# Another order list for an attention and two feed-forward blocks, and the first pair loaded in two parts

## The chip, the cores and the metric

The kernel runs on one core of a Trainium2 chip. The core has TensorE (matrix products and transposes, results in PSUM), VectorE, ScalarE and GpSimd, and SyncE, which here only issues transfers between HBM and the on-chip memory. Each engine takes its instructions from its own queue in order and waits on semaphores for the others. The metric is the device time of the launch in microseconds. The kernel before takes 390.04 us in the median of three runs (389.51 to 390.77).

## The reference

There are 2 sequences of 448 tokens and 12 heads of width 64, all in float32; the weights come as float64.

```
scores = q @ k.T / 8, causal mask, softmax          # per batch and head
x   = (softmax @ v), heads side by side             # 2 x 448 x 768
xp  = x shifted by one token
xk  = mu_k*x + (1-mu_k)*xp ;  xr = mu_r*x + (1-mu_r)*xp
k   = relu(xk @ w_k) ;  v = k*k @ w_v               # 768 -> 1024 -> 768
r   = sigmoid(xr @ w_r) ;  x2 = r*v                 # 768 -> 768
h   = relu(x2 @ w_in)                               # 768 -> 1024
y   = (h * sigmoid(conv3(h, conv_w))) @ w_out       # 1024 -> 768
```

## The kernel before, in words

The attention works on 12 pairs of heads, six per batch. For pair i the steps are: `Lk` and `Lv` (loads of q and k, and of v), `kqT` (14 transposes on TensorE, 7 chunks of 64 tokens of q and of k), `kC` (the two copies out of PSUM), `sc.c` (scores of the query block c, for both heads), `red.c.j` (mask, minimum and scaling on VectorE, head j), `exp` (ScalarE), `rec` (reciprocals of the sums, VectorE), `norm` (scaling by them), `T.a` and `T.b` (transposes of the probabilities), `C.xx` (their copies out of PSUM), `V.kc` (products with v) and `out` (the copy of the result into `xT`).

The linear layers multiply float32 numbers as three products of a high and a low part (`mm3`, L64 to L67). So each activation and each weight slice is split: `mP` and `mD` mix a pair's output with its shifted copy, `mH` and `mL` make its high and low part (`xr`); `kx:P D H L` are the same steps for `xk`. A weight slice of 128 columns comes as float64 and is made float32 by five steps: `wE:L` is its load, `a` runs on ScalarE, `b` to `e` on VectorE (`b` on GpSimd where marked), then `h` and `l` give the two parts. `w0` to `w5` are the slices of w_r, `w6` to `w8` the first three of w_k, named wk0 to wk2 in the profile. There are two raw buffers for such loads; one is free again after step `e`. `pr e.b.c` is one product of slice e with chunk c of batch b, `sr` copies a finished pr result out of PSUM. `E0` and `E1` are the products of the first w_k slice for the two batches, `E2` and `E3` of the second.

All of this up to E3 stands in one list of tokens, `ORDER`, written out by hand or by a search outside the kernel. The loop over it issues each token's instructions in turn, and each engine but SyncE keeps that order exactly; the transfers that SyncE issues keep it among themselves. So a token is held up by whatever stands before it on its own engine. A suffix `/p`, `/a` or `/v` says GpSimd, ScalarE or VectorE. `W0` and `W*n` are matmuls of an identity with itself whose result is never read.

q and k of two pairs fit on chip (`qks` has two buffers): the load of pair i+2 waits for `kqT` of pair i. v has four buffers.

After E3 the other w_k slices, then w_v, w_in and w_out follow in loops (`token_mm`), where the order on each engine is left to the framework's scheduler. `take()` (called once for each slice) issues the conversion of coming slices and returns the next that is ready.

Of the kernel before, what the change touches and what calls it, by code (L numbers as in the profile page):

```python
# [19 lines left out]
def kernel(  # L20
# [233 lines left out]
    class Job:  # L254
        def __init__(self, i):
            self.i, self.b, self.hp = i, i // NPAIR, i % NPAIR
            self.T, self.p, self.s = {}, {}, {}
            self.scored = 0
# [6 lines left out]

        def Lk(self):
            t = self.raw = qks.get(self.i, self.name("rqk"))
            for src, dst, e in ((q, t[:LO], nc.sync), (k, t[LO:], nc.sync if self.i else nc.scalar)):
                for j in range(2):
                    in_order(e.dma_start(  # L270
                        out=dst[:, :, j], in_=src[self.b, 2 * self.hp + j].rearrange("(c p) d -> p c d", p=LO)
                    ))

        def Lv(self):
            t = self.v = vs.get(self.i, self.name("rv"))
            for j in range(2):
                x = v[self.b, 2 * self.hp + j]
                in_order(nc.sync.dma_start(out=t[:, :NB, j], in_=x[:MAIN].rearrange("(c p) d -> p c d", p=P)))
                in_order(nc.sync.dma_start(out=t[LO:, NB, j], in_=x[MAIN:]))

        def kqT(self, _):
            t = self.raw
            pt = {n: bank(self.name(n), 1) for n in "qk"}
            for c in range(S // LO):
                for n, r in (("q", slice(0, LO)), ("k", slice(LO, P))):
                    nc.tensor.transpose(
                        pt[n][:, c * LO:(c + 1) * LO], t[r, c].rearrange("p h d -> p (h d)"), ident[r, r]
                    )
            qks.put(self.i)

        def kC(self, eng, n):
            self.T[n] = t = Ts[n].get(self.i, self.name(f"{n}T"))
            copy(eng, t, used(self.name(n))[:, :S])
# [171 lines left out]
    class Slice:  # L465
# [325 lines left out]
```

## Time and profile before

| | |
|---|---|
| median of three runs | 390.04 us |
| the profiled execution's own time | 390.61 us |
| its span, first to last instruction | 388.7 us |
| TensorE busy, mean granted clock | 366.4 us, 0.987 of 2.4 GHz |
| VectorE, ScalarE, GpSimd busy | 300.5, 228.3, 128.8 us |

All durations below are from this one execution. Matmuls overlap in their pipeline, so a row's duration of one matmul is longer than the distance to the next; a busy TensorE is one that has no gap.

### The profile page before, as it was taken

Reading aid. Unit: us, or ns where it says so; the run is one execution under the profiler, and the core shown is the slowest. Engines: PE = TensorE matmul, PEld = TensorE weight load, DVE = VectorE, ACT = ScalarE, POOL = GpSimd, SP = SyncE. Lnnn points to the kernel's source line nnn. Section 1 sums busy time; section 2 is a strip of 40 time slices with the busy share of each in tenths; the row PEclk is TensorE's granted clock in tenths of the full one; section 3 lists DMA queues with packets and bytes.
Section 4 is the critical chain, followed back from the end, with each engine's and each line's share of the span. In section 5 each row is a group of like instructions: output and inputs, shape, how many; then the busy total and the mean of one; then the engine's idle time right before and its main releaser. Section 6 shows DMA issues by size and latency. Waiting matters only on the chain.

```text
span 388.7 us, 6581 instructions
## 1 busy us (share of the span) xinstructions
PE 366.4 (94%) x2374; PEld 315.5 (81%) x2374; DVE 300.5 (77%) x576; ACT 228.3 (59%) x488; POOL 128.8 (33%) x172
## 2 busy tenths in 40 slices
PE   7886999899896998999999899999999999999996
PEld 6445665576665897999999699999999999999996
DVE  2884999999898899888899799999999999500000
ACT  3984999779724425776778745553777667403111
POOL 2361799786986854100000000000134344300000
PEclk9996999999999999999999899999999999999999
DMA  5548755252213032445535443445521300004111
GB/s 118 126 98 206 193 118 124 80 128 83 83 51 110 3 97 70 160 162 164 193 133 189 142 155 109 146 154 163 162 83 44 118 2 1 2 0 143 41 61 42
DMA packets 60541, 41.36 MB, mean 106 GB/s; under 512 B 34616, under 2 KB 59484, under 8 KB 60508
## 3 DMA queue, kind: packets, MB, share of 16 engines
q1 hardware_dynamic: 59580, 40.71, 35.6%
q8 instruction: 19, 0.31, 0.3%
q10 hardware_dynamic: 928, 0.23, 0.3%
q14 instruction: 14, 0.11, 0.1%
HBM read 38.17 MB, written 2.75 MB: 105 GB/s over the span
## 4 chain that ended last, share of the span: by engine, by line
PE 54%; DVE 19%; DMA 10%; POOL 6%; ACT 6%; issue 3%; SPq 2%; POOLq 0%; ACTq 0%; DVEq 0%
PE pout L66 5%; PE ph L67 5%; PE ph L65 5%; PE ph L66 5%; PE pout L67 5%; PE pout L65 5%; PE pv L66 4%; PE pv L67 4%; PE pv L65 4%; PE s L303 4%; DVE m L415 3%; PE po L383 3%; DMA rqk<-in_k_dram 2%; DVE e L315 2%; POOL m L71 2%
## 5 line engine op out<-in xcount | busy, mean ns | idle before, releaser
L727 POOL TENSOR_TENSOR cv<-cv,hT 128x448 f32<-128x448 f32 x16 | 21.7, 1359 | 156.8 <-ACT cv L726 156.8
L71 POOL TENSOR_SCALAR p<-p,st 128x128 f32<-128x128 f32 (+3 forms) x69 | 40.4, 600 | 32.6 <-DVE st L333 18.9
L324 ACT ACTIVATE p<-e,st 128x384 f32<-128x384 f32 (+3 forms) x84 | 44.0, 527 | 4.4 <-DVE st L315 3.2
L315 DVE CUSTOM_DVE_ANT_0 e<-s,mask 128x256 f32<-128x256 f32 (+3 forms) x84 | 34.6, 444 | 3.9 <-PE s L303 3.3
L303 PE MATMUL s<-kT,qT 64*128 64x128 f32 (+3 forms) x192 | 35.8, 460 | 0.4 <-DVE pt L78 0.4
L756 ACT ACTIVATE osb<-pout 128x384 f32<-128x384 f32 x14 | 6.8, 491 | 40.0 <-PE pout L67 38.8
L415 DVE SCALAR_TENSOR_TENSOR m<-xT,mu,m 128x448 f32<-128x448 f32 x24 | 24.5, 1030 | 4.8 <-POOL m L71 3.5
L383 PE MATMUL po<-pt,rv 128*64 128x448 f32 (+3 forms) x192 | 26.4, 389 | 0.8 <-issue 0.8
L303 PEld LDWEIGHTS s<-kT,qT 64*128 64x128 f32 (+1 forms) x192 | 15.7, 179 | 10.6 <-DVE st L315 3.6
L383 PEld LDWEIGHTS po<-pt,rv 128*64 128x64 f32 (+1 forms) x192 | 12.9, 135 | 13.4 <-issue 8.3
L66 PE MATMUL pout<-wo_t,g 128*128 128x384 f32 x49 | 16.4, 335 | 0.0
L67 PE MATMUL pout<-wo_t,g 128*128 128x384 f32 x49 | 16.4, 335 | 0.0
L65 PE MATMUL pout<-wo_t,g 128*128 128x384 f32 x49 | 16.4, 334 | 0.0
L324 ACT ACTIVATION_READ_ACCUMULATOR p<-e,st 128x1 f32 x84 | 16.1, 191 | 0.0
L90 DVE TENSOR_TENSOR g<-cv,g 128x448 fp32r<-128x448 f32 x16 | 11.6, 725 | 3.7 <-ACT g L86 3.7
L71 POOL TENSOR_SCALAR m<-xT,mu 128x448 f32<-128x448 f32 x16 | 14.0, 879 | 1.1 <-DVE xr L90 0.7
L66 PE MATMUL pout<-wo_u,g 128*128 128x384 f32 x42 | 14.1, 336 | 0.0
L65 PE MATMUL pout<-wo_u,g 128*128 128x384 f32 x42 | 14.1, 335 | 0.0
L67 PE MATMUL pout<-wo_u,g 128*128 128x384 f32 x42 | 14.0, 334 | 0.0
L723 DVE SCALAR_TENSOR_TENSOR cv<-hT,cw,cv 128x448 f32<-128x448 f32 x16 | 13.6, 850 | 0.1
L90 POOL TENSOR_TENSOR xr<-m,xr 128x448 fp32r<-128x448 f32 x10 | 13.0, 1301 | 1.5 <-ACT xr L86 1.2
L722 DVE SCALAR_TENSOR_TENSOR cv<-hT,cw,cv 128x448 f32<-128x448 f32 x16 | 13.0, 812 | 0.4 <-ACT cv L721 0.3
(523 smaller groups left out, 1267.3 us busy)
## 6 DMA issues: line engine op xcount, KB each, us to landing
rqk<-in_q_dram SPq DMA_DIRECT2D x24, 112.0 KB, 3.0
out_dram<-osb SPq DMA_DIRECT2D x14, 192.0 KB, 1.9
rqk<-in_k_dram SPq DMA_DIRECT2D x22, 112.0 KB, 3.0
rv<-in_v_dram SPq DMA_DIRECT2D x24, 96.0 KB, 2.8
wv0raw<-in_moe_w_v_dram SPq DMA_DIRECT2D x1, 1024.0 KB, 5.0
wv1raw<-in_moe_w_v_dram SPq DMA_DIRECT2D x1, 1024.0 KB
wv2raw<-in_moe_w_v_dram SPq DMA_DIRECT2D x1, 1024.0 KB
wv3raw<-in_moe_w_v_dram SPq DMA_DIRECT2D x1, 1024.0 KB
```

Of the source, the lines that this page charges most:

```text
L65: nc.tensor.matmul(ps_out, lh, rh, start=first, stop=False)
L66: nc.tensor.matmul(ps_out, lh, rl, start=False, stop=False)
L67: nc.tensor.matmul(ps_out, ll, rh, start=False, stop=last)
L71: nc.gpsimd.tensor_scalar(out_, in_, s, 1.0, ALU.mult, ALU.mult)
L90: e.tensor_tensor(out_, x, f32(h), ALU.subtract)
L303: nc.tensor.matmul(o, qT[r, c * P:min(S, (c + 1) * P)], kT[r, :w], start=True, stop=True)
L315: nc.vector.tensor_tensor_reduce(t[:, :w], used(self.name(f"s{c}{j}"))[:, :w], mask[:, MAIN - w:] if c < NB else mask2, -SCALE, 3e38, ALU. ...
L324: nc.scalar.activation(p, self.s[c, j][:, :w], AF.Exp, bias=self.st[:, 0, i:i + 1], scale=-1.0, accum_out=self.st[:, 1, i:i + 1],)
L383: nc.tensor.matmul(self.po[j * D:(j + 1) * D, kc * P:S], self.v[r, kc, j], self.T["pt"][r, a:a + n], start=kc == 0, stop=kc == NB,)
L415: nc.vector.scalar_tensor_tensor(m, xT[c][:, b, 1:S + 1], mu[:, a:a + 1], m, ALU.mult, ALU.add)
L723: nc.vector.scalar_tensor_tensor(a, hT[:, 2:S + 2], cw[:, 2 * NF + f:2 * NF + f + 1], a, ALU.mult, ALU.add)
L727: nc.gpsimd.tensor_tensor(a, a, hc, ALU.mult)
```

## The change

The list is another one throughout: the same tokens in another order, some on other engines, and with 13 more of the unread matmuls (23 instead of 10). The loads of pair 0 are cut: part A is chunks 0 and 1 of q (SyncE) and of k (ScalarE's queue); the other five chunks follow, all from SyncE. Its transposes and copies are cut in the same way (`kqTA`, `kCA`, `kqTB`, `kCB`). The tails of v (the last 64 tokens) of both heads of a pair come in one transfer instead of two. In the loop over the w_v slices the sigmoid of `sr[e]` stands before `take()` instead of behind it.

```diff
+        CUT = 2
+        CHUNKS = {"": (0, S // LO), "A": (0, CUT), "B": (CUT, S // LO)}
...
+        def rows(self, c0, c1):
+            for src, dst, e in ((q, self.raw[:LO], nc.sync), (k, self.raw[LO:], nc.scalar if c1 == self.CUT else nc.sync)):
+                for j in range(2):
+                    x = src[self.b, 2 * self.hp + j, c0 * LO:c1 * LO]
+                    in_order(e.dma_start(out=dst[:, c0:c1, j], in_=x.rearrange("(c p) d -> p c d", p=LO)))
+
+        def LkA(self):
+            self.raw = qks.get(self.i, self.name("rqk"))
+            self.rows(0, self.CUT)
+
         def Lk(self):
-            t = self.raw = qks.get(self.i, self.name("rqk"))
-            for src, dst, e in ((q, t[:LO], nc.sync), (k, t[LO:], nc.sync if self.i else nc.scalar)):
...
+            if self.i:
+                self.raw = qks.get(self.i, self.name("rqk"))
+            self.rows(0 if self.i else self.CUT, S // LO)
...
-                in_order(nc.sync.dma_start(out=t[LO:, NB, j], in_=x[MAIN:]))
...
+            in_order(nc.sync.dma_start(out=t[LO:, NB], in_=x[:, MAIN:].rearrange("j p d -> p j d")))
...
-        0:Lk W0 0:kqT 0:kC.q/v 0:kC.k/a W*3 0:sc.0 0:red.0.0 0:sc.1 0:exp.0.0 0:red.0.1 0:red.1.0 0:exp.0.1
-        0:exp.1.0 1:Lk 0:red.1.1 1:kqT 2:Lk 1:kC.q/v 0:sc.2 0:sc.3 0:red.2.0 1:kC.k/a 0:red.2.1 1:sc.1 1:sc.2
...
-        pr4.1.2 k7:D w6:c w8:L w6:d w6:e sr3.0/v k3:H/a pr3.1.5 sr1.0/v pr4.1.3 w6:h k3:L/v k11:P/a k7:H/p pr5.0.3
-        w6:l/p k7:L/p sr5.1/v w8:a pr4.1.4 k11:D w7:h pr4.1.5 pr5.0.4 k11:H/a w8:b/v w8:c k10:D w8:d w7:l/v pr4.0.5
-        k10:H/a sr4.0/v pr5.0.5 w8:e w8:h sr4.1/a k10:L/p k11:L/v E0 E1 E2 sr5.0/a sr3.1/a w8:l/p sr0.1/v E3
+        0:LkA 0:Lk W0 0:kqTA 0:kCA.q/v 0:kCA.k/a W*1 0:sc.0 W*8 0:kqTB 0:red.0.1 0:kCB.q/a 0:kCB.k/v 0:red.0.0 1:Lk
+        W*3 0:sc.1 0:red.1.1 0:red.1.0 0:exp.0.1 0:sc.2 0:exp.0.0 0:exp.1.1 0:red.2.0 0:red.2.1 W*1 1:kqT 0:exp.1.0
+        0:sc.3 1:kC.q/v 1:kC.k/a 0:exp.2.0 W*1 1:sc.0 0:exp.2.1 0:red.3.0 1:red.0.1 1:red.0.0 0:rec.a 0:norm.2.0/p
+        0:exp.3.0 1:exp.0.0 1:sc.1 1:sc.2 2:Lk sm:L 1:exp.0.1 1:red.1.1 1:red.1.0 0:rec.b 0:norm.0.0/p 2:kqT
...
+        w8:b/v pr5.1.5 k7:D pr4.0.3 pr4.0.4 sr3.0/v k7:H/p k7:L/v w7:c w8:c sr5.0/a pr4.0.5 k9:L/p w7:d w8:d w7:e
+        w7:h w7:l/p w8:e w8:h w8:l/p pr4.1.5 E0 E1 sr4.0/v sr5.1/v E2 E3 sr4.1/a
...
     for e in range(NE):
-        w = take()
         x2.append(big(f"X{e}", f"x2_{e}"))
         tc.keep_in_program_order(nc.scalar.activation(sr[e], sr[e], AF.Sigmoid))
+        w = take()
```

The transfers stand in this order in the old list: Lk of pairs 0, 1, 2 and 3, Lv of 1, the small vectors (`sm:L`, three issues), Lk of 4, Lv of 0, 4 and 2, Lk of 5. In the new one: Lk of pair 0 in two parts, Lk of 1 and 2, `sm:L`, Lk of 3 and 4, Lv of 0, Lk of 5, Lv of 1, Lk of 6.

On other engines than before, by count (old to new): k copies on VectorE 7 to 1 and q copies 5 to 3, beside pair 0's parts; short copies `C.1` and `C.3` on VectorE 21 to 24 and long ones `C.a` 8 to 10; `out` on VectorE 2 to 4; `sr` 7 to 5; low parts on GpSimd 18 to 12, on VectorE 6 to 12; high parts on GpSimd 16 to 10; `P` steps on GpSimd 16 to 12; step `b` on GpSimd 5 to 4; `norm` on GpSimd 69 as before but for the choice of blocks, on VectorE 7 to 8.

## Rows read from the trace of the kernel before

**Rows 1.** The page: engines, busy us (share of the span) and instructions
```profile
PE 366.4 (94%) x2374; PEld 315.5 (81%) x2374; DVE 300.5 (77%) x576; ACT 228.3 (59%) x488; POOL 128.8 (33%) x172
```

**Rows 2.** Stages of the span: length, busy us (instructions) by engine, TensorE's clock, transfers
```profile
0.00:6.80 6.80, 4.36 (x29) 4.03 (x29) 0.00 (x0) 1.28 (x1) 2.18 (x12) 1.00 0.64 135
6.80:27.40 20.60, 19.02 (x212) 11.29 (x212) 17.33 (x77) 17.48 (x60) 8.60 (x18) 1.00 0.49 110
27.40:34.30 6.90, 2.73 (x36) 2.03 (x34) 2.28 (x11) 2.76 (x10) 1.54 (x3) 0.73 0.75 193
34.30:40.40 6.10, 6.10 (x49) 3.86 (x49) 4.83 (x17) 4.61 (x16) 3.04 (x7) 0.75 0.86 175
40.40:100.00 59.60, 56.79 (x642) 38.41 (x641) 58.68 (x183) 52.84 (x163) 48.83 (x68) 1.00 0.45 114
100.00:146.20 46.20, 40.85 (x221) 34.36 (x219) 41.18 (x51) 18.29 (x30) 35.53 (x34) 1.00 0.25 76
...
154.10:210.00 55.90, 55.36 (x273) 51.35 (x274) 49.40 (x68) 40.95 (x68) 2.24 (x1) 1.00 0.49 160
210.00:220.00 10.00, 8.64 (x37) 6.97 (x36) 8.91 (x11) 8.63 (x12) 0.00 (x0) 0.91 0.48 156
```

**Rows 3.** The same columns for the time just after the stop
```profile
33.00:37.30 4.30, 4.30 (x49) 3.63 (x45) 2.15 (x8) 2.53 (x6) 0.00 (x0) 0.50 1.11 255
```

**Rows 4.** Timeline of TensorE: start, us, line, operation [idle before, what ended it]
```profile
5.80 0.34 PE L286 MATMUL q<-ident,rqk 64*128 64x64 f32 x1 [0.35 <-DMA rqk<-in_q_dram]
...
6.75 0.94 PE L559 MATMUL W<-ident 128*128 128x128 f32 x6
...
30.99 0.33 PE L286 MATMUL q<-ident,rqk 64*128 64x64 f32 x1 [3.01 <-DMA rqk<-in_q_dram]
32.48 0.34 PE L286 MATMUL k<-ident,rqk 64*128 64x64 f32 x1 [1.16 <-DMA rqk<-in_k_dram]
```

**Rows 5.** Timeline of SyncE's queue of transfers, 0 to 30 us
```profile
0.73 3.03 SPq L270 DMA_DIRECT2D rqk<-in_q_dram  x4
...
12.96 0.50 SPq L279 DMA_DIRECT2D rv<-in_v_dram  x1
...
27.48 1.29 SPq L270 DMA_DIRECT2D rqk<-in_q_dram  x2
```

**Rows 6.** Timeline around the end of the list: VectorE, GpSimd and TensorE
```profile
153.10 0.94 DVE L145 SCALAR_TENSOR_TENSOR wk2c<-wk2raw,wk2c 128x768 int32<-128x768 int32 x1
...
155.06 2.24 POOL L90 TENSOR_TENSOR wk2hl<-wk2c,wk2hl 128x768 fp32r<-128x768 f32 x1 [3.23 <-ACT wk2hl L86]
...
155.15 0.36 PE L65 MATMUL pk<-xk,wk1hl 128*128 128x448 f32 x1
```

**Rows 7.** VectorE copies out of PSUM by form: count, busy us, mean ns
```profile
L78 DVE COPY pt<-Yb 128x256 f32<-128x256 f32 x12 | 4.9, 417 | 0.1
...
L78 DVE COPY kT<-k 128x448 f32<-128x448 f32 x7 | 4.3, 613 | 0.0
...
L78 DVE COPY pt<-Xa 128x512 f32<-128x512 f32 x4 | 2.8, 688 | 4.6 <-PE Xa L349 4.6
```

**Rows 8.** Steps of the mixes to 160 us: count, ns min/median/max, first, last start
```profile
L415 DVE SCALAR_TENSOR_TENSOR m<-xT,mu,m x24: 672/1006/1570, 50.5 to 149.3; 128x448 f32<-128x448 f32 x24
...
L90 POOL TENSOR_TENSOR xk<-m,xk x8: 1142/1278/1738, 115.4 to 150.6; 128x448 fp32r<-128x448 f32 x8
...
L90 DVE TENSOR_TENSOR xk<-m,xk x4: 611/616/1579, 124.8 to 154.0; 128x448 fp32r<-128x448 f32 x4
...
L71 POOL TENSOR_SCALAR m<-xT,mu x16: 632/639/1793, 40.7 to 139.5; 128x448 f32<-128x448 f32 x16
```

**Rows 9.** VectorE's waits from 100 to 146.2: us, times, longest
```profile
DVE m L415 <- POOL m L71: 3.5, 4, 1.1
```

**Rows 10.** Timeline around the first w_v slice: ScalarE, then TensorE
```profile
211.31 1.28 ACT L698 ACT_TABLE_LOAD   x1
...
216.99 0.47 PE L65 MATMUL pv<-k,wv0hl 128*128 128x448 f32 x1 [0.97 <-ACT k L86]
```

More of the change, by code (lines that the diff above doesn't have):

```diff
@@ L278, in Lv, with kqT @@
-                in_order(nc.sync.dma_start(out=t[:, :NB, j], in_=x[:MAIN].rearrange("(c p) d -> p c d", p=P)))
-                in_order(nc.sync.dma_start(out=t[LO:, NB, j], in_=x[MAIN:]))
-        def kqT(self, _):
+                in_order(nc.sync.dma_start(out=t[:, :NB, j], in_=x[j, :MAIN].rearrange("(c p) d -> p c d", p=P)))
+            in_order(nc.sync.dma_start(out=t[LO:, NB], in_=x[:, MAIN:].rearrange("j p d -> p j d")))
+        def kqT(self, _, h=""):
             t = self.raw
-            pt = {n: bank(self.name(n), 1) for n in "qk"}
-            for c in range(S // LO):
+            pt = {n: bank(self.name(n + h), 1) for n in "qk"}
+            for c in range(*self.CHUNKS[h]):
@@ L285, in kqT @@
                 for n, r in (("q", slice(0, LO)), ("k", slice(LO, P))):
[L286 to L293, printed above, removed]
+                    o = (c - self.CHUNKS[h][0]) * LO
+                    nc.tensor.transpose(pt[n][:, o:o + LO], t[r, c].rearrange("p h d -> p (h d)"), ident[r, r])
@@ new lines, in kqT, with kqTA, kqTB, kC @@
+            if h != "A":
+                qks.put(self.i)
+        def kqTA(self, _):
+            self.kqT(_, "A")
+        def kqTB(self, _):
+            self.kqT(_, "B")
+        def kC(self, eng, n, h=""):
+            if n not in self.T:
+                self.T[n] = Ts[n].get(self.i, self.name(f"{n}T"))
+            o, z = (c * LO for c in self.CHUNKS[h])
+            copy(eng, self.T[n][:, o:z], used(self.name(n + h))[:, :z - o])
+        def kCA(self, eng, n):
+            self.kC(eng, n, "A")
@@ new lines @@
+        3:norm.0.1/p 4:red.1.0 3:norm.2.0/p 1:out/v 5:sc.0 3:norm.3.0/p 4:red.1.1 5:sc.2 3:norm.1.1/p 2:C.aY/a
+        5:red.0.0 4:exp.2.0 3:norm.2.1/p 3:norm.0.0/p 5:red.2.0 w1:L 4:exp.1.0 5:red.0.1 6:kqT 4:rec.a 4:exp.1.1
+        6:kC.k/a 5:red.2.1 3:T.b 4:rec.b 3:T.a 3:Lv 1:mP/p 5:sc.1 1:mD 2:V.0 6:kC.q/a 5:exp.2.0 2:V.1 2:V.2
+        4:norm.2.0/p 2:V.3 5:exp.0.1 3:C.3X/v 5:exp.2.1 7:Lk 5:red.1.0 5:exp.0.0 4:Lv 5:sc.3 5:exp.1.0 4:norm.2.1/p
+        4:norm.1.1/p 3:C.3Y/a 4:norm.1.0/p 2:out/a w1:a 3:C.1Y/v 3:C.aY/v 5:red.1.1 3:C.aX/v 6:sc.3 4:norm.0.0/p
@@ new lines @@
+        6:sc.0 4:norm.0.1/p 5:red.3.0 5:exp.1.1 4:T.a 1:mH/p 5:rec.a 3:C.1X/a 6:sc.2 6:red.0.0 6:sc.1 5:exp.3.0
+        4:norm.3.0/p 6:red.0.1 4:C.aY/v 7:kqT 6:red.2.0 4:C.aX/a 6:red.1.1 4:T.b 5:norm.0.1/p 6:exp.0.0 6:exp.2.0
+        3:V.0 7:kC.q/a 0:mD 7:kC.k/a 3:V.1 8:Lk 3:V.2 5:rec.b 4:C.3Y/a 5:norm.2.1/p 6:exp.1.1 3:V.3 6:red.2.1
+        4:C.3X/v 4:C.1X/v 5:norm.0.0/p 6:red.3.0 w1:b/p 6:exp.2.1 6:red.1.0 1:mL/p 6:exp.0.1 5:norm.2.0/p 7:sc.1
+        5:T.a 3:out/a 6:exp.3.0 7:sc.2 4:C.1Y/v 5:norm.1.0/p w1:c 8:kqT 7:red.1.1 5:norm.3.0/p 5:norm.1.1/p 9:Lk
@@ new lines @@
+        6:exp.1.0 2:mP/p 4:V.0 5:C.aX/v 7:red.2.1 6:rec.b 6:rec.a 4:V.1 7:red.2.0 7:red.1.0 8:kC.q/a 7:exp.2.1 4:V.2
+        5:Lv 8:kC.k/a 5:C.aY/a 5:T.b 8:sc.0 7:sc.0 4:V.3 7:exp.2.0 w1:d 5:C.1X/v 5:C.3X/a 8:red.0.0 7:sc.3 0:mH/p
+        7:exp.1.1 10:Lk 7:red.0.0 4:out/v 6:norm.2.1/p 6:norm.0.1/p 7:red.0.1 6:Lv 6:norm.0.0/p 6:norm.3.0/p
+        7:exp.1.0 9:kqT 7:exp.0.0 8:sc.2 5:C.3Y/v 7:exp.0.1 6:norm.2.0/p 8:red.0.1 6:T.a 7:Lv 7:red.3.0 9:kC.k/a
+        9:kC.q/a 5:C.1Y/v 6:norm.1.1/p 8:red.2.1 8:sc.1 7:exp.3.0 2:mD 6:norm.1.0/p 6:C.aX/a 6:T.b 7:rec.a 7:rec.b
@@ new lines @@
+        6:C.3X/v 6:C.3Y/a 8:red.1.1 5:V.0 6:C.1Y/v 8:exp.2.1 5:V.1 3:mP/p 7:norm.2.1/p 8:red.2.0 11:Lk 6:C.aY/a
+        8:exp.0.1 8:exp.1.1 5:V.2 7:norm.2.0/p 9:sc.3 5:V.3 8:sc.3 8:red.1.0 7:norm.1.0/v 8:exp.2.0 8:exp.0.0 3:mD
+        6:C.1X/a 9:sc.1 9:red.3.0 w0:L 7:norm.0.0/p 7:norm.0.1/p 8:exp.1.0 2:mH/p 9:red.1.0 7:norm.1.1/p
+        7:norm.3.0/p 8:rec.a 10:kqT 5:out/a 8:red.3.0 9:sc.2 w1:e 10:kC.q/a 8:Lv w2:L 10:kC.k/a 0:mL/p 7:T.a 11:Lv
+        8:exp.3.0 7:T.b 6:V.0 7:C.1X/v 6:V.1 8:rec.b 7:C.3X/v 7:C.3Y/v 7:C.aY/a 6:V.2 9:exp.1.0 w1:h 6:V.3 9:red.2.1
@@ new lines @@
+        9:red.1.1 7:C.aX/v 9:sc.0 7:C.1Y/a 8:norm.0.0/p 9:red.0.0 8:norm.0.1/p 4:mP/p 9:exp.2.1 8:norm.1.1/p 10:sc.2
+        8:norm.3.0/p 9:red.0.1 11:kqT 6:out/a 4:mD 8:norm.1.0/p 9:exp.1.1 8:T.b 9:exp.3.0 9:exp.0.0 8:norm.2.0/v
+        8:norm.2.1/p 7:V.0 9:red.2.0 8:C.3X/a 9:rec.b 11:kC.q/a w1:l/v 7:V.1 3:mH/a 7:V.2 8:C.1X/a 11:kC.k/a
+        10:red.2.0 7:V.3 8:C.1Y/v w0:a 7:out/v 10:red.2.1 8:T.a 2:mL/p 8:C.aY/a 9:norm.1.0/p w0:b/v 10:sc.0 8:C.3Y/v
+        w0:c 9:exp.0.1 10:red.0.1 5:mP/p 9:Lv pr1.0.0 pr1.0.1 pr1.0.2 w0:d 8:C.aX/a 10:sc.1 9:norm.3.0/a
@@ new lines @@
+        10:C.3Y/a 11:norm.2.1/a 11:norm.1.0/p 9:V.2 11:norm.2.0/v 10:C.1Y/a 11:norm.3.0/p 11:norm.0.0/v 9:V.3
+        10:C.aY/a 11:norm.0.1/v 10:C.aX/a 8:mH/p 11:T.b 11:C.1X/a 11:C.3X/a 8:mL/v 11:T.a 11:C.1Y/v 9:out/a k4:D
+        w5:b/p 10:V.0 10:V.1 10:V.2 11:C.aY/a w3:h 11:C.aX/v 11:C.3Y/v 11:V.0 9:mP/a 11:V.1 11:V.2 10:V.3 11:V.3
+        7:mH/a w3:l/v act2 w4:L pr3.0.0 9:mD 7:mL/v pr3.1.0 pr2.1.1 w5:c 11:out/v w4:a pr0.1.0 pr0.1.1 9:mH/a k4:H/a
+        9:mL/v 10:out/a pr0.1.2 pr2.1.2 k5:P/a w5:d pr3.0.1 10:mP/a w4:b/p 10:mD w5:e 10:mH/a pr0.1.3 pr2.1.3 k4:L/p
```

99 lines of the change are left out of this document (34 added, 65 removed).

## The prediction

> **What bounds the kernel now.** I read the page's busy times first, then the span cut into stages, then TensorE's own waits and the loading queue behind the longest of them, then the durations of what the new list moves from engine to engine, and last the two places where the ordered part hands over to the rest. The page [rows 1] says TensorE is busy 94% of 388.7 us, so about 22 us of idle time is what an order can win at most, plus time at the lower clock. The stages [rows 2] say where it lies. From 154.1 to 210 TensorE is full (55.36 of 55.90) and so, but for the tail, is the end of the kernel: nothing there is touched. Before that, four places. To 6.8 us VectorE has nothing. From 27.4 to 34.3 everything stands: TensorE 2.73 of 6.90, VectorE 2.28, and TensorE's granted clock is at its lower level, 1.2 GHz, from 33.0 to 37.3 (0.50 [rows 3], where it is 1.00 from 40.4 on). From 40.4 to 100 VectorE is the bound: 58.68 of 59.60. From 100 to 146.2 both have gaps, TensorE 5.35 us and VectorE 5.02, while GpSimd is busy 35.53 of 46.20.
>
> The stop at 27.4 is a load that comes late [rows 4]: pair 5's q transposes wait 3.01 us and k's 1.16 more, to 32.48. SyncE began to issue it only at 27.48 [rows 5], because its queue works through one issue after another, some 0.65 us each, from 0.73 on, and 37 issues stand before pair 5's: 2 of pair 0, 4 each of pairs 1 to 4, 4 each of v of pairs 1, 0, 4 and 2, and 3 small ones. 37 by 0.65 from 0.73 on is 24.8, and the rest of the way to 27.48 are waits for buffers.
>
> The handover at the end of the list: the last VectorE step of the list, the fifth of wk2's conversion, runs from 153.10 to 154.04, and its low part is there 3.26 us later, at 157.30 (155.06 + 2.24). TensorE starts on wk1's slice (E2) at 155.15 [rows 6]. From there the rest takes 390.6 - 155.15 = 235.4 us, with 390.61 the profiled execution's own time. Its execution was 0.6 above the median 390.04.
>
> **The change, part by part.** *Loads.* The new list puts 28 issues before pair 5's: 6 of pair 0 (2 in part A, 4 in the rest, whose k now also goes by SyncE), 16 of pairs 1 to 4, 3 small, 3 of pair 0's v, whose tail is one issue instead of two (0.50 saved for each of 12 pairs [rows 5]). 28 by 0.65 from 0.73 is 18.9; with the 2.7 us of buffer waits that the old queue had, 21.6 at the latest. From the first issue to the use of k it took 5.0 us (27.48 to 32.48), so pair 5 is there at 23.9 to 26.6. TensorE reached pair 5 at 28 before, and has 2.5 us more work in front of it now, so the stop should go. Worth for VectorE: the 7.11 us that it did from 27.4 to 40.4 would take 8.46 at its pace of 6.8 to 27.4 (17.33 of 20.60 [rows 2]) and 7.2 at that of 40.4 to 100, instead of 13.0: 4.5 to 5.8. I take **-5.2**. What is late next: for pairs 6 to 11 the list has 3.8 us (pair 8) to 12.9 us of VectorE work between load and transposes, by the durations of [rows 7, 8] and their like, so 8 and 9 have little to spare, and the engines themselves come next.
>
> *Pair 0 in two parts.* Its transposes began at 5.80, 0.35 after TensorE ran out of warming matmuls [rows 4]. Part A is two of seven chunks, so scores of block 0 can begin earlier; at best by the 1.3 us that two issues take. Against it, four more issues (2.6 us) stand on SyncE before pair 1's, pair 0's second part and eight warming matmuls (three take 0.94 us [rows 4], so about 0.3 each, 2.4 in all) lie before its other blocks, and pair 2's load, which waits for pair 0's buffer, is late by as much. Bounds -1.3 and +2.6; I take **0**, since VectorE is idle 6.8 us at the front and catches up on the part that it gets early. The 13 added warming matmuls are 3.9 us of TensorE, nearly all before pair 5. From 6.8 to 27.4 it was idle only 1.6 us [rows 2], so the cover is its wait for the others' results and is thin: they cost 0 to 3.9 on TensorE's own path, weighed below.
>
> *Work moved between engines.* VectorE gives up 12 q and k copies for four whole ones and two parts, about 6.7 of 0.61 us, and two sr copies, 5.3 us in all; it gets 3 more short pt copies (0.42), 2 long ones (0.69), 2 output copies (0.61), 6 low parts of the mixes (0.61 to 1.58), one clamp and one scaling, about 0.5 each by the short copy [rows 7, 8]. With the low parts at 0.62 that is 8.6, so **+3.3** (+9.1 with all at 1.58). ScalarE takes some 7.5 us, most of it after 100 us where it was busy 18.29 of 46.20. GpSimd loses 6 low parts at 1.28 and 11 scalings, splits and clamps at 0.64 [rows 8]: 14.7 us, most of it behind the sixth pair's share. That matters to VectorE: the mix step at L415 takes 0.67 at best and 1.01 in the median of 24, and the same low part 0.61 or 1.58, while GpSimd runs its own; of its 5.02 us of gaps from 100 to 146.2, 3.5 are waits for GpSimd's first mix step [rows 9]. Bounds of this relief 0 and 7.6 (all gaps, and a third of L415's 8 us of stretch); I take half of it, **-3.8**.
>
> The Trainium skill speaks against the moved low parts. Its page "SBUF — State Buffer", section "Who interferes with whom", says that a VectorE instruction with two inputs in SBUF and a GpSimd one that reads SBUF lock each other out for a whole instruction. The 0.61 and 1.58 of the same subtraction [rows 8] fit it; what it would make of the sum is the third rival.
>
> *The end of the list.* In the old list wk1's fifth step stands 46 tokens before wk2's; in the new one 3 before, both at its very end, so E2 depends on it. List end 154.0 + 3.3 - 5.2 - 3.8 + 0 = 148.3; wk1's fifth step ends 0.94 before, 147.4; low part 3.3 later, 150.7: E2 starts at **150.7 instead of 155.15, 4.45 earlier**. TensorE's own path: without 4.17 us of idle and with the 4.3 us at 0.50 done in half, 6.3 less, plus 0 to 3.9 of warming, brings E2 to 148.8 to 152.7 by itself. So the two paths are close, and VectorE's is taken.
>
> *Sigmoid before the next slice's conversion.* There the list does not rule. At 211.31 a table load (1.28) and then the sigmoid lie on ScalarE ahead of the last k2 squares; TensorE waits 0.97 at 216.99 [rows 10], 1.36 idle from 210 to 220, and after it runs at 1.2 GHz for a while (clock 0.91 in that window [rows 2], so 0.9 us lost there and about as much after 220). Earlier at best all of that goes, -3; if the table load falls between other late steps, as much as itself and the sigmoid, +2.2. Nothing in the old trace says which: **0**.
>
> Sum: 390.6 - 4.45 = **386.1 us**, 3.9 under the median of the runs.
>
> **The rivals.** *Better:* TensorE's path rules (E2 at 148.8), and the wait at 217 goes: 390.6 - 6.35 - 3 = 381.2. For it: VectorE's waits from 100 on are for GpSimd. Against it: it asks for every gap to close. *The split buys nothing:* part A lands hardly sooner, since the first load takes as long as a whole one, and all later loads are 2.6 us late: E2 at 153.3, 388.7 us. For it, the queue's one-after-another issues from the first us on. *Contention:* the five or six low parts cost VectorE the long duration each, five times 0.97 us, 4.8: E2 at 155.5, 390.9, no change. The 1.58 speaks for it [rows 8]; GpSimd's 10.7 us of gaps from 100 to 146.2, with 14.7 us less to do, speak against it. (It is what the Trainium skill's rule above would make of these steps.) *Slower:* E2 waits for wk1's low part. Place: the first products of wk1 behind the last steps of the list on VectorE. With no relief, the stop worth only 4.5 and the start 2.6 late, the list ends at 154.0 + 3.3 - 4.5 + 2.6 = 155.4, E2 is at 157.8 and the time 393.2. It decides as soon as wk1's fifth step ends after 151.9; in the old list its place before wk0 kept it from ever deciding.
>
> **How the numbers follow.** Forecast 0.48, with its own range 383.5 to 388.3; better 0.14; split buys nothing 0.14, a third of it above the line for no change; contention 0.10; slower 0.14. A measurement of this kernel tells about 0.3% (1.2 us) from no change: faster 0.71, same 0.15, slower 0.14. The range 380 to 391.5 leaves out a third of the better case and most of the slower one, and takes in both ends of the start and of the relief.
>
> **What would show it.** Right: no TensorE wait over 1 us for a q or k load after 10 us, its clock at 1.00 from 30 to 40; VectorE's gaps from 100 to the first wk1 products well under 5 us and a median of L415 under 1.0; those products at 150 to 151.5. Wrong: a wait for pair 1 or 2's load, or wk1's first products waiting for their low part past 153; a new wait of TensorE after 155 for a conversion; a longer wait around the first wv slices.

## The result, and the profile after

The changed kernel takes **378.28 us** (median of 4 runs, 376.5 to 379.6), beside 390.4 of the kernel before on the same chip: 0.967 of it, 95% interval 0.959 to 0.975. Run again twice, on two chips, it took 378.1 both times (0.973, 0.967 to 0.979, and 0.973, 0.969 to 0.977). The forecast was 386.1 with a range of 380.0 to 391.5: the direction was right, the gain a third of what came. (The diff printed above has one token wrong: pair 0's first k copy is `0:kCA.k/v`, on VectorE, so that VectorE makes three part copies for pair 0 and not the two that the prediction counted.)

The profiled execution took 378.69 us, span 376.9. Its page, engines line:

```profile
PE 367.5 (98%) x2400; PEld 318.0 (84%) x2400; DVE 295.6 (78%) x584; ACT 234.0 (62%) x499; POOL 109.1 (29%) x155
```

TensorE does as much as before [rows 1] in 11.8 us less. GpSimd lost 19.7 us of busy time. VectorE, which by the prediction's count was given 3.3 us more work, is busy 4.9 us less. The stages, with the columns of [rows 2]:

```profile
6.80:27.40 20.60, 20.60 (x206) 14.03 (x206) 14.45 (x66) 14.85 (x51) 7.73 (x17) 1.00 0.54 121
27.40:34.30 6.90, 6.52 (x100) 4.59 (x95) 6.68 (x28) 6.47 (x23) 3.05 (x6) 1.00 0.63 138
34.30:40.40 6.10, 5.97 (x81) 4.00 (x77) 5.62 (x27) 5.37 (x18) 4.61 (x10) 1.00 1.10 251
...
100.00:146.20 46.20, 46.20 (x266) 39.94 (x262) 43.70 (x59) 25.87 (x46) 19.99 (x21) 1.00 0.21 66
...
210.00:220.00 10.00, 10.00 (x51) 9.26 (x51) 9.31 (x15) 5.25 (x9) 0.00 (x0) 1.00 0.62 212
```

The stop at 27.4 is gone (VectorE 6.68 instead of 2.28), the clock is 1.00 in every stage shown, and TensorE has no gap in this profile from 100 to 146.2 (40.85 busy before) and none at 217. In the waits of TensorE over the whole span (total, times, longest) no single wait behind the first, at the start, is over 0.6 us:

```profile
PE W L584 <- POOL xT L216: 2.1, 1, 2.1
PE s L327 <- DVE st L339: 1.3, 3, 0.6
PE po L407 <- DVE st L339: 0.6, 1, 0.6
```

The mix step on VectorE, to be held beside L415 in [rows 8] (ns min/median/max):

```profile
L439 DVE SCALAR_TENSOR_TENSOR m<-xT,mu,m x24: 669/684/2258, 40.5 to 138.2; 128x448 f32<-128x448 f32 x24
```

The median exaggerates the gain. What adds up is the sum, and here are busy us and mean ns of the same 24 steps, then VectorE's idle time just before them and what ended most of it, first in the kernel before, then in the changed one:

```profile
L415 DVE SCALAR_TENSOR_TENSOR m<-xT,mu,m 128x448 f32<-128x448 f32 x24 | 24.5, 1030 | 4.8 <-POOL m L71 3.5 <-ACT m L75 1.3
L439 DVE SCALAR_TENSOR_TENSOR m<-xT,mu,m 128x448 f32<-128x448 f32 x24 | 21.3, 894 | 1.6 <-POOL m L71 1.5
```

Where the 11.8 us of span went is read from four marks on TensorE's timeline: the first product of wk0 (the first that needs `xk`), of wv0 (line "pv"), of the w_in layer, and the end.

| profile | first wk0 | to first wv0 | to first w_in | to the end |
|---|---|---|---|---|
| before | 146.20 | 60.0 | 62.1 | 120.3 |
| after | 138.28 | 59.2 | 58.4 | 121.1 |
| after, second profile | 135.56 | 59.8 | 58.4 | 121.9 |

7.9 us (10.6 in the second) come before wk0, 3.8 between the first wv0 and w_in products, where the wait and the low clock of [rows 10] and [rows 2] stood. The other stretches together change by 0.1 in the first profile and take 1.3 longer in the second.

### The profile page after: what moved, and what is told of

Same layout as the page of the kernel before. It is cut to its first block, busy times and chain, and to the rows that moved or that the text cites. A ratio compares the mean times of both kernels' runs of the same rounds, so it can differ in the third digit from the quotient of the medians.

```text
span 376.9 us, 6650 instructions
## 1 busy us (share of the span) xinstructions
PE 367.5 (98%) x2400; PEld 318.0 (84%) x2400; DVE 295.6 (78%) x584; ACT 234.0 (62%) x499; POOL 109.1 (29%) x155
## 4 chain that ended last, share of the span: by engine, by line
PE 34%; DVE 33%; DMA 14%; ACT 11%; issue 5%; POOL 2%; ACTq 0%; SPq 0%; POOLq 0%; DVEq 0%
PE pout L66 5%; PE pout L67 5%; PE pout L65 5%; PE ph L66 5%; PE ph L67 5%; PE ph L65 4%; DVE e L339 4%; DVE m L439 4%; ACT p L348 3%; DVE pt L78 3%; PE W L584 3%; PE s L327 2%; DMA wk4raw<-in_moe_w_k_dram 2%; DMA wv5raw<-in_moe_w_v_dram 2%; DMA wv3raw<-in_moe_w_v_dram 1%
## 5 line engine op out<-in xcount | busy, mean ns | idle before, releaser
L752 POOL TENSOR_TENSOR cv<-cv,hT 128x448 f32<-128x448 f32 x16 | 23.3, 1456 | 153.4 <-ACT cv L751 153.4
L348 ACT ACTIVATE p<-e,st 128x128 f32<-128x128 f32 (+3 forms) x84 | 44.2, 530 | 5.7 <-DVE st L339 4.8
L71 POOL TENSOR_SCALAR p<-p,st 128x384 f32<-128x384 f32 (+3 forms) x69 | 37.3, 558 | 32.1 <-DVE st L357 21.7
L339 DVE CUSTOM_DVE_ANT_0 e<-s,mask 128x384 f32<-128x384 f32 (+3 forms) x84 | 35.1, 444 | 3.0 <-PE s L327 2.3
L439 DVE SCALAR_TENSOR_TENSOR m<-xT,mu,m 128x448 f32<-128x448 f32 x24 | 21.3, 894 | 1.6 <-POOL m L71 1.5
L66 PE MATMUL pout<-wo_t,g 128*128 128x384 f32 x49 | 16.4, 335 | 0.0
L65 PE MATMUL pout<-wo_t,g 128*128 128x384 f32 x49 | 16.4, 334 | 0.0
L86 ACT ACTIVATE g<-cv 128x448 fp32r<-128x448 f32 x16 | 9.2, 578 | 10.2 <-POOL cv L752 9.7
L71 POOL TENSOR_SCALAR m<-xT,mu 128x448 f32<-128x448 f32 x12 | 10.1, 840 | 15.0 <-DVE xk L90 7.1
L66 PE MATMUL pout<-wo_u,g 128*128 128x384 f32 x42 | 14.1, 336 | 0.0
L65 PE MATMUL pout<-wo_u,g 128*128 128x384 f32 x42 | 14.1, 335 | 0.0
L584 PEld LDWEIGHTS W<-ident 128*128 128x128 f32 x46 | 9.0, 286 | 4.8 <-issue 2.5
```

What stands on the lines that cost most here:

```text
L65: nc.tensor.matmul(ps_out, lh, rh, start=first, stop=False)
L66: nc.tensor.matmul(ps_out, lh, rl, start=False, stop=False)
L71: nc.gpsimd.tensor_scalar(out_, in_, s, 1.0, ALU.mult, ALU.mult)
L339: nc.vector.tensor_tensor_reduce(t[:, :w], used(self.name(f"s{c}{j}"))[:, :w], mask[:, MAIN - w:] if c < NB else mask2, -SCALE, 3e38, ALU. ...
L348: nc.scalar.activation(p, self.s[c, j][:, :w], AF.Exp, bias=self.st[:, 0, i:i + 1], scale=-1.0, accum_out=self.st[:, 1, i:i + 1],)
L439: nc.vector.scalar_tensor_tensor(m, xT[c][:, b, 1:S + 1], mu[:, a:a + 1], m, ALU.mult, ALU.add)
```

## The experiments

Medians are beside the kernel before on the same chip, whose median was 388.4 to 389.9 in the five series. The kernel before is called the old list, the changed one the new list.

**1. Pair 5's load early, old list.** `5:Lk` moves up behind `0:Lv`, ahead of v of pairs 4 and 2.

```diff
-4:Lk 0:Lv ... 4:Lv ... 2:Lv ... 5:Lk
+4:Lk 0:Lv 5:Lk ... 4:Lv ... 2:Lv
```

> The old list with one token moved: pair 5's load stands before pair 4's and pair 2's v instead of behind them, eight issues (some 5 us) earlier on SyncE; nothing else changes. Theory of parts: the stop from 27.4 to 34.3 goes, TensorE's clock stays at 1.00 there, and VectorE, which was idle 4.6 us of it, wins 4.5 to 5.8: 384.5 to 386. Rival, the list as a whole: the work behind the stop runs earlier but loses the time again at the next late load or at the old list's gaps from 100 us on: 388 to 390.

388.1 us, 0.997 (0.993 to 1.001), as the rival said. Pair 5 comes at 27.2, but another stop takes the place of the first (stages, columns as before):

```profile
27.40:34.30 6.90, 6.12 (x78) 3.62 (x76) 4.45 (x19) 3.39 (x11) 4.48 (x10) 1.00 0.80 200
34.30:40.40 6.10, 4.49 (x41) 3.68 (x43) 3.82 (x13) 5.75 (x20) 1.55 (x3) 0.61 0.93 193
```

ScalarE's timeline says why (idle before, what ended it):

```profile
33.68 0.89 ACT L136 ACTIVATE wr2c<-wr2raw 128x768 f32<-128x768 f32 x1 [3.34 <-DMA wr2raw<-in_moe_w_r_dram]
```

The first weight slice of the list is late too. Its conversion stands in ScalarE's queue ahead of the exponentials of the next block, so VectorE and then TensorE stand. In the kernel before this second late load was hidden behind the first.

**2. Only the engines of the mixes, old list.** 30 `P`, `H` and `L` tokens take the engine that they have in the new list, the order untouched. On GpSimd that makes 4 scalings, 6 high parts and 6 low parts fewer; ScalarE gets the scalings and high parts, VectorE the low parts.

```diff
-3:mH/p 5:mH/p 9:mP/p 7:mL/p k1:L/p ...
+3:mH/a 5:mH/a 9:mP/a 7:mL/v k1:L/v ...
```

> The old list in its old order, with each mix step (first step, high part, low part, for xr and xk) on the engine that the new list gives it; 14 us leave GpSimd, 4 to 6 us come to VectorE, some 7 to ScalarE. Theory of parts: VectorE's gaps from 100 to 146 shrink and its mix steps shorten, 1 to 4 us faster: 386 to 389. Rival, list as a whole: the steps now meet an order that was made for other engines, ScalarE's queue holds them up, no gain or up to 2 us slower: 390 to 392.

383.8 us, 0.989 (0.983 to 0.995): 5.3 us, more than any theory had. The stage and the mix step:

```profile
100.00:146.20 46.20, 44.24 (x237) 37.38 (x236) 45.15 (x61) 24.30 (x41) 21.92 (x22) 1.00 0.27 86
```

```profile
L415 DVE SCALAR_TENSOR_TENSOR m<-xT,mu,m x24: 665/686/1576, 49.8 to 143.7; 128x448 f32<-128x448 f32 x24
```

```profile
L415 DVE SCALAR_TENSOR_TENSOR m<-xT,mu,m 128x448 f32<-128x448 f32 x24 | 20.8, 879 | 0.8 <-POOL m L71 0.6 <-ACT m L75 0.2
```

GpSimd falls from 35.53 to 21.92 us busy, and TensorE gains 3.4 us in this stage. The mix step, with the same code, sums to 20.8 us instead of 24.5, and VectorE's waits before it to 0.8 instead of 4.8.

**3. Only the sigmoid's place, old list.** The wait for the weight (`take()`) goes behind the sigmoid.

```diff
-        w = take()
         x2.append(big(f"X{e}", f"x2_{e}"))
         tc.keep_in_program_order(nc.scalar.activation(sr[e], sr[e], AF.Sigmoid))
+        w = take()
```

> The old kernel with the one edit outside the list: the sigmoid's call stands before take(). The framework's order on ScalarE then has the last k2 squares and copies ahead of the table load and the sigmoid, as in the new kernel. Theory: TensorE's 1.36 us of waits at the first w_v slice go, and the lower clock after them (0.91 and 0.92 in two windows of 10 us, 1.7 us): 3 us faster, 387. Rival: the list's lateness on VectorE is what TensorE waits for there, and the wait stays: 390.

386.9 us, 0.995 (0.992 to 0.999), as expected. TensorE is full at 217 and its clock stays up:

```profile
210.00:220.00 10.00, 10.00 (x51) 9.26 (x50) 8.30 (x10) 7.41 (x11) 0.00 (x0) 1.00 0.44 157
```

**4. The changed kernel again.**

> The new kernel unchanged, on the same chip as the three single parts: both theories 377 to 379. The sum of the three parts against its 12 us says how much of the gain needs the new order itself: theory of parts 9 to 12 of it, rival under 5.

378.1 us; its profile is the third row of the table of marks.

**5. The old engines of the mixes, new list** (experiment 2's tokens the other way round).

> The changed kernel, with the engines of the P, H and L mix steps put back to those of the list before (GpSimd gets its share back), the order untouched. The edit alone on the old list was worth 5.3 us (0.9887 of the kernel before). Theory, that GpSimd's relief is the largest part of the gain also here: slower than the changed kernel (378.2) by 3 to 6 us, 381 to 384 us, with GpSimd's busy time in 100 to 140 us near 30 us and TensorE no longer full in the window before the list's end. Rival, that the new order has places for GpSimd's steps as well and the engines matter little in it: 378 to 379.5 us.

383.9 us, 0.987 (0.982 to 0.991), as the theory said. GpSimd's relief is worth some 5.7 us here (378.1 to 378.3 with it), about as on the old list, and the new order without it brings 5.7 us by itself. The stage, and VectorE's waits in it:

```profile
100.00:146.20 46.20, 41.42 (x211) 35.20 (x208) 38.86 (x42) 17.78 (x29) 35.63 (x30) 1.00 0.16 52
```

```profile
DVE m L439 <- POOL m L71: 3.4, 3, 2.3
DVE m L439 <- ACT m L75: 2.3, 3, 1.2
DVE wr4hl L90 <- ACT wr4hl L86: 1.1, 1, 1.1
```

At the end of the list two conversion steps of wk1 and wk2 run beside GpSimd's low parts and take twice their time. GpSimd's and VectorE's timelines here, then VectorE's of the changed kernel, where GpSimd is idle at that place (140.61 to 145.59):

```profile
143.84 3.16 POOL L90 TENSOR_TENSOR xk<-m,xk 128x448 fp32r<-128x448 f32 x2
144.09 1.90 DVE L143 SCALAR_TENSOR_TENSOR wk1c<-wk1raw,wk1c 128x768 int32<-128x768 int32 x1
145.91 1.90 DVE L143 SCALAR_TENSOR_TENSOR wk2c<-wk2raw,wk2c 128x768 int32<-128x768 int32 x1
```

```profile
141.95 0.95 DVE L143 SCALAR_TENSOR_TENSOR wk1c<-wk1raw,wk1c 128x768 int32<-128x768 int32 x1
142.82 0.95 DVE L143 SCALAR_TENSOR_TENSOR wk2c<-wk2raw,wk2c 128x768 int32<-128x768 int32 x1
```

**6. Pair 0 whole, new list.** `0:LkA`, `0:kqTB` and the second copies go, the rest of the list stays.

```diff
-0:LkA 0:Lk W0 0:kqTA 0:kCA.q/v 0:kCA.k/v W*1 0:sc.0 W*8 0:kqTB ...
+0:Lk W0 0:kqT 0:kC.q/v 0:kC.k/a W*1 0:sc.0 W*8 ...
```

> The changed kernel with pair 0 loaded, transposed and copied whole, as before; its extra products on the identity stay. Theory, that the split is worth little, because in the changed kernel the second part stands behind eight extra products (10.95 us) and pair 1's transposes come at 14.0 us against 8.4 before: within 1 us of the changed kernel, 377.5 to 379.2 us, and pair 0's transposes near 5.8 us. Rival, that the split carries the start: 380 us or more.

377.2 us, 0.971 (0.966 to 0.976): the split buys nothing.

**7. Without the 13 added products on the identity, new list.**

```diff
-W*1 0:sc.0 W*8 0:kqTB ... W*1 1:kqT
+0:sc.0 0:kqTB ... 1:kqT
```

> The changed kernel without its 13 added products on the identity (W*8 and five W*1; W*3 stays, as before). They take 3.78 us at 7.24 us and 0.45 to 0.5 us each later, about 6 us of TensorE's time in the first 27 us. Theory, that they pay by keeping TensorE at its upper clock level until the work is dense (granted clock 1.00 in every stretch of the changed kernel, 0.50 in a part of the kernel before): a stretch below 1.00 appears in the first 40 us and the time rises by 1 to 3 us, 379 to 381 us. Rival, that they only delay the second part of pair 0: pair 0's second part comes some 3.5 us earlier and the time falls by 1 to 3 us, 375 to 377 us. Nothing: within 1 us, when VectorE's sum decides at the list's end whatever the start does.

375.9 us, 0.966 (0.962 to 0.970), and beside the changed kernel on one chip:

> The changed kernel once more, on the same chip as the next run, so that the two stand side by side: 377.5 to 378.5 us, 0.967 to 0.973 of the kernel before.

> The changed kernel without its 13 added products on the identity, beside the changed kernel on one chip. Theory, that these products lie on TensorE's own path, which rules up to the list's end (full from 100 to 146 us): 1.5 to 3 us under the run beside it. Rival, that the 2.3 us between the earlier two runs were the difference of two chips: within 1 us of it.

378.1 (0.973, 0.969 to 0.977) with them, 376.6 (0.969, 0.964 to 0.973) without: 1.5 us, twice in the same direction, with intervals that overlap. They don't pay; that they cost 1 to 2 us is likely, not shown. Without them the granted clock from 5.6 to 11.0 was 1.00 in one profile and 0.76 in the other, and neither run was slower than with them.

**8. Three parts together, old list** (1, 2 and 3).

> The kernel before with three parts of the change together: pair 5's load issued earlier, the mix steps on the new engines, the sigmoid ahead of the wait for the weight. One by one they gave 1.0, 5.3 and 2.2 us. Theory, that they lie in three different stretches and add: about 380.7 us (380 to 382), 8.4 us under the kernel before, leaving 2.5 us to the new order and its start. Rival, that the load stop is given back at the list's end once GpSimd no longer delays VectorE, or the other way round: 382.5 to 384 us, hardly under the mix engines alone (383.8).

383.4 us, 0.984 (0.980 to 0.989), as the rival said: no better than the mix engines alone within the intervals. ScalarE waits 3.31 us for the weight slice, and the clock is 0.62:

```profile
34.30:40.40 6.10, 4.17 (x38) 3.53 (x40) 3.83 (x13) 6.06 (x20) 1.90 (x4) 0.62 0.91 179
```

**9. Both 6 and 7, new list.**

> The changed kernel without its 13 added products on the identity and with pair 0 loaded whole, both at once. Alone they gave 375.9 (without the products) and 377.2 us (whole), against 378.2 of the changed kernel. Theory, that the products' time at the start is the loss and the split brings nothing: 374.5 to 376 us, not slower than without the products alone. Rival, that the split pays once nothing stands between its two parts: 376.5 us or more.

376.7 us, 0.969 (0.963 to 0.974): not told apart from either alone.

**10. The sigmoid's place undone, new list** (experiment 3's edit the other way round).

> The changed kernel with the edit at the sigmoid undone (the wait for the weight ahead of the sigmoid again), all else as changed. On the old list this edit gave 2.2 us. Theory, that the changed list already puts the last squares of the mix (k2) ahead of the table load on ScalarE, so that TensorE does not wait at the first pv products whichever stands first: 377.5 to 379 us. Rival, that the edit carries its part here too: 380 to 382 us, with a wait of about 1 us near the second pv products and a granted clock under 1.00 after it.

377.4 us, 0.974 (0.967 to 0.980): no difference. The edit that gave 2.2 us on the old list gives nothing here, because the last squares of k come ahead of the table load without it too. ScalarE's timeline of this run:

```profile
199.90 0.57 ACT L713 ACTIVATE a<-a 128x448 f32<-128x448 f32 x1
200.51 0.58 ACT L86 ACTIVATE k<-a 128x448 fp32r<-128x448 f32 x1
...
202.05 1.28 ACT L723 ACT_TABLE_LOAD   x1
```

In the kernel before the table load (211.31 [rows 10]) stood ahead of the last two.

**11 and 12. Work for GpSimd that nobody waits for, new list.** 30 multiplies on a tile of their own in GpSimd's idle places between 100 and 146 us; then 120 fills of two elements a row in the same places.

```diff
+            nc.gpsimd.tensor_scalar(junk, junk, 1.0, 1.0, ALU.mult, ALU.mult)   # 128x256, 30 times
+            nc.gpsimd.memset(junk[:, :2], 0.0)                                  # instead, 120 times
```

> The changed kernel with 30 added multiplies on GpSimd over a 128x256 float tile of their own (about 0.4 us each by 128x448 at 0.63, some 12 us together), in the stretches between 100 and 146 us in which GpSimd is idle; nothing depends on them. Theory, that GpSimd's work slows VectorE's while it runs: VectorE's steps of the mix get longer (median 684 ns in the changed kernel, 1006 in the kernel before), and the list ends 2 to 5 us later: 380 to 383 us. Rival, that GpSimd's old share cost time only because VectorE and TensorE waited for its results: VectorE's durations stay and the time is within 1 us of the changed kernel.

> As the run before, with 120 fills of two elements a row (about 0.1 us each, so about 12 us of GpSimd's time) in the places of the 30 multiplies: as much of GpSimd's queue, hardly any data. Theory, that it is the data which slows VectorE: within 1 us of the changed kernel (377.5 to 379.2), VectorE's steps of the mix at a median near 684 ns. Rival, that the occupied queue delays GpSimd's own steps: as late as the run with the multiplies.

384.8 us (380.7 to 387.5) with the multiplies, 0.988 (0.983 to 0.992); 376.5 with the fills, 0.970 (0.965 to 0.976). GpSimd is occupied by both, by the fills 5 us less (39.11 and 34.34 us busy from 100 to 146.2, 19.99 in the changed kernel), and VectorE's mix steps wait for GpSimd for 1.5 and 1.6 us. What the multiplies change is VectorE's durations; groups of its instructions from 100 to 147 us, busy us and mean ns, with the multiplies:

```profile
L90 DVE TENSOR_TENSOR xr<-m,xr 128x448 fp32r<-128x448 f32 x5 | 3.8, 751 | 0.0
...
L143 DVE SCALAR_TENSOR_TENSOR wk1c<-wk1raw,wk1c 128x768 int32<-128x768 int32 x1 | 1.1, 1140 | 0.0
...
L141 DVE TENSOR_SCALAR wk0c<-wk0c 128x768 int32<-128x768 int32 x1 | 0.8, 755 | 0.0
...
L78 DVE COPY sr<-pr 128x448 f32<-128x448 f32 x1 | 0.6, 611 | 0.0
```

and with the fills:

```profile
L90 DVE TENSOR_TENSOR xr<-m,xr 128x448 fp32r<-128x448 f32 x4 | 2.5, 637 | 0.0
...
L78 DVE COPY sr<-pr 128x448 f32<-128x448 f32 x3 | 1.8, 608 | 0.0
...
L143 DVE SCALAR_TENSOR_TENSOR wk1c<-wk1raw,wk1c 128x768 int32<-128x768 int32 x1 | 0.9, 946 | 0.0
...
L141 DVE TENSOR_SCALAR wk0c<-wk0c 128x768 int32<-128x768 int32 x1 | 0.6, 556 | 0.0
```

The low parts and these conversion steps, all of them on SBUF, take 18 to 36% longer with the multiplies than with the fills; the copies out of PSUM don't. The last conversion step of the list on VectorE ends at 148.0 with the multiplies and at 143.1 with the fills. (The Trainium skill's page "SBUF — State Buffer", section "Who interferes with whom", says that a VectorE instruction with two inputs in SBUF contends with a GpSimd instruction that reads SBUF and not with one that only writes it. The two runs agree with it for the two-input steps at L90 and L143, which were as short with the fills as in the changed kernel. For L141, which has one input, they don't show why it got longer.) The theory holds, and the medians put more than its price on it: 8.3 us over the fills, 6.6 over the changed kernel (in the profiled executions, whose spans are 381.3, 377.6 and 376.9, about 4).

**13 and 14. Both late loads early, old list.** `w2:L` follows `5:Lk`, with the three parts of experiment 8 and alone.

```diff
-4:Lk 0:Lv ... 5:Lk ... w2:L
+4:Lk 0:Lv 5:Lk w2:L ...
```

> The kernel before with the three parts of the earlier run (pair 5's load early, the mix steps on the new engines, the sigmoid first) and one more: the load of the weight slice w2 issued right behind pair 5's. In the run of the three parts, ScalarE waited 3.31 us for that slice (its first conversion at 34.0), the softmax and the output transposes stood behind it in ScalarE's queue, and TensorE waited 2.2 us at a granted clock of 0.62: the stop had moved from the one load to the other. Theory, that the half of the gain which the new order brings by itself is above all these late loads: 379.5 to 381.5 us, 2 to 4 us under the three parts (383.4), and the clock 1.00 from 34 to 40. Rival, that the order helps elsewhere: 383 to 384 us, given back before the list's end.

> The kernel before with pair 5's load and the load of w2 early, and nothing else changed. Pair 5's alone gave 1.0 us (0.9969 of the kernel before). Theory, that the stop goes as a whole only when both are early: 4 to 5 us under the kernel before, some 385 us. Rival, that VectorE's and GpSimd's old load takes the gain back before the list ends, as it did with the one load: 387.5 to 389 us.

380.4 us, 0.980 (0.975 to 0.985), and 385.7, 0.992 (0.989 to 0.996). With the three parts the second load is worth 3.0 us by the medians and 1.8 by the two ratios, whose intervals overlap. The clock in the stage is back, and less of the stop is left (VectorE 4.51 of 6.10, 5.62 in the changed kernel):

```profile
27.40:34.30 6.90, 6.59 (x81) 3.90 (x79) 6.74 (x29) 6.73 (x22) 4.38 (x9) 1.00 0.70 172
34.30:40.40 6.10, 4.97 (x73) 3.78 (x74) 4.51 (x20) 4.75 (x18) 3.15 (x7) 1.00 0.59 129
```

Alone the two loads give 2.6 us, between theory and rival. So four edits bring the old list to 380.4, which is 8.0 of the 10.4 to 12.1 us that separate the kernels.

## Why the prediction was wrong, step by step

*Loads.* The stop went as forecast: no wait for q or k after 10 us in the changed kernel, the clock at 1.00. By 40.4 VectorE had done 27.2 us of work, 24.4 before: 2.8 us, where the step had 5.2. The difference is the start, which came later (VectorE 14.45 from 6.8 to 27.4, 17.33 before); in the second profile, with a faster start, it is 4.5. On the old list the step would have been wrong, since it priced this stop as if nothing stood behind it: experiments 1 and 8 show a second late load there, with a wait of 3.3 us, which the trace before shows only as 0.52 us at 35.62 on ScalarE.

*Pair 0 in two parts*, taken as 0: right (experiment 6). Its second part waited at 10.95 behind the eight products, and pair 1 came at 14.0 instead of 8.4. The rival that the split buys nothing was right on the split, and wrong that the time would then be 388.7.

*Work moved between engines*: **this step failed.** It set +3.3 us on VectorE against a relief of 3.8, together -0.5; the engines of the mixes alone gave -5.3 on one list and -5.7 on the other. What was mis-sized is the relief, of which the step took half of its bound of 7.6. On the old list (experiment 2) the whole of it came: VectorE's waits before the mix step fell by 4.0 us and the mix step itself by 3.7. The six low parts that VectorE got there cost 4.0 us (12 instead of 6 of them, 9.6 us instead of 5.6), near the 3.7 that the step had. On the new list (experiment 5 against the changed kernel) the waits fell by 4.0 as well (5.6 to 1.6), the mix step only by 1.5 (22.8 to 21.3); there conversion steps shortened too, by 0.95 us each the two shown above, which the step had left out. The experiments on the mix engines don't separate waiting from stretching. The third rival, in which each moved low part takes 1.58 us, did not come: a few do (1.32, 1.57 and 2.25 us among the 7 of `xk` in the changed kernel), but the six together cost 0.7 each in experiment 2 and 0.9 in the changed kernel.

*The end of the list*: **failed too.** E2 was put at 150.7 and began at 145.71, which is 5.0 of the 7.4 us that the profile stands under the forecast. Two errors make it up. wk1's fifth step ended at 144.64 instead of 147.4, 2.8 earlier: the 5.2 by which the step before was short, less the 2.4 that the loads were short of theirs. And E2 does not need wk1's low part to begin, for which the step had added 3.3 us. It needs the high part, which ScalarE had ready 0.9 after the fifth step. ScalarE's, TensorE's and GpSimd's timelines of the changed kernel:

```profile
144.67 0.85 ACT L86 ACTIVATE wk1hl<-wk1c 128x768 fp32r<-128x768 f32 x1 [6.84 <-DVE wk1c L145]
```

```profile
145.71 0.37 PE L65 MATMUL pk<-xk,wk1hl 128*128 128x448 f32 x1
145.92 0.36 PE L66 MATMUL pk<-xk,wk1hl 128*128 128x448 f32 x1
146.50 0.47 PE L65 MATMUL pk<-xk,wk2hl 128*128 128x448 f32 x1 [0.22 <-ACT wk2hl L86]
...
147.49 0.47 PE L67 MATMUL pk<-xk,wk1hl 128*128 128x448 f32 x1
```

```profile
145.59 1.84 POOL L90 TENSOR_TENSOR wk1hl<-wk1c,wk1hl 128x768 fp32r<-128x768 f32 x1 [4.98 <-ACT wk1hl L86]
```

The products at L65 and L66 use the high part of the weights alone, and wk2's stand in between until wk1's low part was there at 147.4. So the slower rival had no place. The step's other path, TensorE's own, was also put too late (148.8 to 152.7): it gained 6.3 us before the added products, from the stop's 4.17 us and the half clock. But TensorE was idle 13.9 us from 6.8 to 146.2 before [rows 2] and 3.1 after, which is 10.8, and with 2.2 for the 4.3 us at 1.2 GHz [rows 3] that makes 13.0. The two paths stayed as close as the step had them: the high part was there at 145.52 and TensorE came free at 145.71, and in the second profile E2 waits 0.46 us for the high part. The rival called better, which asked for TensorE to be full, came nearest.

*Sigmoid*, taken as 0: 3.8 us in the profiles between wv0 and w_in, the other large miss. Its wait and low clock were read rightly, and -3 was given as the best case. On the old list the edit is worth 2.2 us in the medians (experiment 3); on the new list it is worth nothing (experiment 10), because there the squares come before the table load anyway. The order on ScalarE is not the whole cause either. In experiments 1 and 14 the table load stands ahead of the last two squares as before (at 207.83 and 205.89), and TensorE waits only 0.2 us for a low part there, at a clock of 1.00. The last square is ready 9.0 us after wv0's first product in both, 10.7 in the kernel before; why it came later there is not shown.

Sum: 386.1 less 5.0 (E2) less 3.8, plus 1.4 that later stretches took longer, is the profile's 378.7. What stays open is 2 to 4 us: the new list against the old one with four edits (experiment 13), the changed kernel being 0.967 to 0.973 and that one 0.980. No single token was found for it, and the profiles don't place it: the one of experiment 13 is the fastest of its six executions, with a span of 377.1 beside 376.9 and 375.6 of the changed kernel.

## What to carry to other kernels

When steps leave GpSimd, price two things in full: the waits of VectorE for them, and the stretch of VectorE's steps on SBUF that ran beside them. The stretch shows beforehand as the sum of one instruction form over its count times the minimum, and its median can mislead. When a stop of all engines is removed, look along each queue for the next load or wait that the stop was hiding. And at a handover, look up which part of an operand the first product reads, and sum all gaps of the engine that ends last over the whole stretch before it.

## What the runs showed beside this

The eight products on the identity after the first scores took 3.78 us in one profile of the changed kernel and 2.05 in its two others, with a granted clock of 1.00 from 5.6 to 11.0 in all (TensorE's timeline, first the slow one, then the second profile):

```profile
7.24 3.78 PE L584 MATMUL W<-ident 128*128 128x128 f32 x16
```

```profile
6.85 2.05 PE L584 MATMUL W<-ident 128*128 128x128 f32 x16
```

That is 236 and 128 ns each. So at the very start the granted clock of a stretch does not tell which speed the products had, and the start of one and the same kernel differs by 2 us between executions (pair 1 at 14.0 and 11.9).
